# Splitting the second-half query projection 288/224 instead of 256/256, with a new written order

## The chip, the cores and the metric

The kernel runs on one core of one Trainium2 chip. The metric is device time in microseconds; lower is better. The core has five engines that run side by side and wait for each other by semaphores: TensorE (PE, with PEld for its weight loads), VectorE (DVE), ScalarE (ACT), GpSimd (POOL) and SyncE (SP), which here only starts DMAs.

## What is computed

Two attention layers share one input and their outputs are mixed by a gate. Layer A is recurrent: the 2048 rows are cut into 64 segments of 32, each is joined with 8 memory rows, and the first 8 rows of its output are the memory of the next segment.

```python
for s in range(64):                       # A: S=2048, Dm=512, H=32, Dh=128, M=8
    h = concat([mem, x[:, 32*s:32*s+32]])         # 40 rows
    q, k, v = h @ Wq, h @ Wk, h @ Wv              # 32 heads of 128
    p = softmax(where(mask, q @ k.T * Dh**-0.5, -1e9))
    o = (p @ v) @ Wo
    mem = o[:, :8]; outs.append(o[:, 8:])
# B: 4 blocks of 512 rows, 32 heads of 16: causal softmax attention in the block,
#    mixed with a linear-attention memory carried from block to block
g = sigmoid((x * gate_w).sum(-1))
return g * a + (1 - g) * b
```

The memory chains the 64 segments of A one behind the other. B does not wait for A, and fills gaps.

## The kernel before

**Work of a segment.** `p_seg(s)` records the operations of one segment. Heads come in two halves, r = 0 and r = 1, of 16 heads. `project(kind, r, ...)` records a projection through `wproj` (line L1391): for each of 4 chunks of the 512 input features it issues 4 matmuls, which work side by side on four 32-column strips of the array, with the same 32 rows of `h` (24 new rows and the 8 of the memory) as weights and up to 512 columns of the weight matrix streaming. The result, 128 partitions by up to 512 columns in one PSUM bank, is evicted to a buffer `st` in bf16 (`copy`, line L997, on ACT or DVE). For keys and queries `ktr` then turns 32x32 blocks on DVE (line L1447) into `KT` and `QT`. Values are evicted to `V_sb` alone.

The queries of half 1 are the one projection in two pieces: `two` gives the column ranges, and the names of the second piece's operations end in b: q1 and q1b on PE, their evictions, their transposes. Each piece has its own PSUM bank, eviction and transpose, and can be ordered apart from the other.

The rest of a segment, for each half r:

- H (a mask, 224 columns, line L1020) and S (scores, L1462 and L1466) into one bank; S_1 reads KT and both pieces of QT of half 1.
- exp on ACT (L1470), U (sums over keys, L1485), ln and rc on ACT (L1489, L1491: the reciprocal as exp of minus ln), then nrm on DVE (L1493) and nrr on DVE or POOL (L1496), which scale the probabilities.
- PV (L1527, L1532) and eviction of O into `OT_sb` (L997, `OTev`).
- wo, 8 steps of output projection (L1296), their eviction `par`, fold (a small matmul), and `hm` on DVE (L1319), which writes the memory rows of the next segment's `h`.

**Work beside it.** The other 8 rows of each segment, which depend on no memory, are projected for four segments at a time (rv, rk, rq of groups j, also L1391, with `xr` as weights). Each goes through one of three staging buffers `stg`; the values take a way through DRAM (rvst, L1363: `rest_v<-stg`). A projection's first matmul also waits until its staging buffer is free. Their output projection is wor (L1296, `OTr_sb`). Layer B has its own logits (bL, L1137), exponentials (bE, L1155), masks (bM, POOL), values (bPV, L1178) and tail (brow, `fin`, output DMAs). Pieces of its logits share four PSUM banks with the PV of half 1. `blast` is the last row block's B product.

**What sets the order.** Operations are recorded with their reads and writes and a set of candidate engines. The order of each engine's instructions is not found when the kernel is built: `ORDER`, a compressed string, lists for each of PE, ACT, DVE, POOL and SP which operation comes next, and `schedule()` follows it (`sequences()`, `given()`). An operation that may run on ACT or DVE (every `copy`), or on DVE or POOL (nrr), runs where the list has it. PSUM banks are handed out in the course of that. Each engine runs its list strictly in order; an instruction waits for the operations that it depends on, and with it all that stand behind it. PE runs either with four column strips, four row strips or the whole array, operation by operation.

Of the kernel before, what the change touches and what calls it, by code (L numbers as in the profile page):

```python
# [15 lines left out]
    "c-nPZ2S5|o8~<J|$z?$jP_ZJ40xsNWRkRLp)veS~_o{nUaqoenYNd|4t#uU_RdJ!<#syWXsEGa@sMV^7KuCb(-u>UZth->rgmCxno4@b(eedCLt<2<IfOKZvG@C-U41d%r"  # L16
    "mcsZ=<2SC%GMMGpZ@~!d(}c*RDMfo``kr{tbb{q(So3eSy%*XP-d(hC_4rlR>aRX6PQ5f|Y5x}1=y|j1-QE_G1(R#^sc~)pr}^lEsqzP-DaWU1g(4;+bjI8jvktY+4#+;$"
    "DZSpAq>;tHpKG_jf8vMzlVYYCURDBA(W!yYy&&$dt4SRIPD96z;S1&QJpq#7_G!**?ra&JyZlI6hsJ%Uri8az+$JpTW|ONeZUEGK^%0=rtB_)qH^7Zx-zwL8WEhzA`eopQ"
    "R%N-`@Ja_T89%|3uORR_Tm<<3!2E-)Ex>~CbrtGsO?RLNLX0-g`*x_;t?(RBSyZx=aJbRt!Z!~(zi}>wK0cdOzfI&69HRv}SWP}T0IKDC0I~xVfzKaV;7XKBZUS^UYaOMq"
    "BF5Xqf(1Y$&sE7D252>@<^788239kJD!rbt^b8brKLZe@uqv!<n-thQwh#=tDg@B*FLjOkS8mJ$rNe@W0KZIP;uWYEmCXZCK=He(j0Ij){U3xDUT^j6B|ux(;+x%$Hz^08"  # L20
    "BnImXbY{&z{_-5Je6?AZ9iYxU)VpdWc<XY_A7UrJ>VH|Muqe2^07VHA<l|$tf(bwuJG(FzqT{lcx}3WY5L)?UTaMA^A)OpP$E?XwLm}uu{j$P$<o=&7x#s~QlXj+ZtTq>U"
    "&z=W58^e53n}3Nh!Lr4Nccus;o7^NT|ArQM4R;O8<rucuOHq<9Cpr852gb&LQg(sd@BIA^P&thyA@7)><;*&U%ku~MvjB$qsD~-5h`9}4liSbYtixS#h#%g2>nMP8h~e~#"
    "9G%%aPt9hQeP8Ki8Qtmy_m56f#z69Imv4Om{s<0BL<o5m7)uZXxjs4il0sm>CujX!*5%pX6X3F`fx^O+Eza{T$*51^pefW9=rqf|8dP);V4O>2b_@TMN(2E2mHmLUN+>de"
    "+N?I~xy<@^p<H};3XJ##V46$xvHRWX90(m`2b$tD7(Wp}5;(xNNw(i7y2Q?3s^2~tG03X7s4Qw(fgyL@tQ7#u3P{dbm-k92Rua_;j`OjBoPfq)El|b6kD9`@Fw^bM&93ju"
    "9v{Ln#OrrKPoK8X6dLab7ivwft7%Q3OwaN8#-(=|tkS-zF!omkLI=haaNhE~zP|?Ls0pBDnLS^ape8&aX3Teqo<?3jbxE#b2LUm`E8noMmps2sYDu%HYwz3kuX^s1eVe?("
    "^m|8>@FOjliM6>b5Z5(@O1G^(<n^IjinoA2M)eG!92hJzu$gtx4DQ(CW3tGjs-UNI@!Wd7=N#i0hVv~38uxXJip=5P%_S0-EUgCck4yD#2x)fx@s&gxDm|FJV9ZLR#jI|3"
    "jKI1HTzxiZPjz>+_QCpI(Zh&Gd0fN)nL`1dvN@p6@il3+1DBKm<*RF>GD6KTa<3Cpr$3)An#8eIz2bwn8QSj(wdO;+%kT}P$<nIBBWP*1qdO@Q&L=~g3o-GjM-icqZL{oV"
    "gO*t`+bWOmKX=g*SnA5|7zIGA*RX>W1|+{`&=DADNztrYIC|r|ZSIBlKvwI4tqTc+u{h70)Bpf0mlerF$h{Z8z}Ow+=V+II^lD~xI5LPSX0@?{3o4?YdoB9KXT?;=(-cC&"
    "2m*=Y*>h;<md>N=4`npyzTk*OD4OH_X^I(J31Ni8!_*sL6rl^K?~<LC-7^J-Fq~CuHRdbp-vkAMIvI=&)RkdH)H|WRomOW71bh9}fm3+pGCG0=6`QMxUMT}m+v*UzD?fBn"
    "!uUUX{Q26y`!S7T#WcdAY!O@Zw*1?!k24_vkg|Bkh#eCP=dYYe>TRt{cna*=e&ozq0rNU}o@RY?&d%X#vz9=kHe|XhC;;H)>Cx6=Qjb)yyZ~6%Y8y#-qThB9!SW_FF*V>="  # L30
    "nTnv??3Mqtku_fhW?gQDLghO+G1Ub$WAwWBWeKm+`ZgBBi{Q^bIg}6HLfz(P*`g=o(#=k{Na?IT@YgAl-O5i`+D5csW%osy&kc<6>%$f;FoL@`M1PDrvMcVaow;<#1okFE"
    "%hzq=nQzmf8zDmKUA|HN30MZK^3%O+?a9q#m#j*#zFQ?qSjabrl%eJsR44E@zpDzGzk`&g$%?M7wSN$N$0;Xj3yD}Susl`;7%b_kfb5WTwYeT>Z5EnEQU0sE1}I`bHbiC}"
    "N1LM}pZsf@&d3@hdp)fkNFtFQqCU{n6|O4)AG_-l`m)8unmif=)#k~hmu?)talG2LHV*DeiDBRw9Vr}ro<e2O+19~~qLmW}D?e&j_z3F6KZHeg!>6qQ_;F{SZ9haNopX^5"
    "=%4t@I0~=y&<yfxJ(rWyJ44H8fL*jCy}<nSEfU;D_v+k3p%<aD?G;h%7x=soYCg9&r~&(4&xjgqCvXA<vRG?{li!nAlmlmSg8-fczhOy5GAw*nl6J=u-71+0{7B`fg*Bw{"
    "wLZ5$nM?+)&y_7Ebw7_FkMKLRN(*~fs60LgUb^Bmfb_T)UZ?sBcs7=p2?em92q#1E6Lp1`D=8Ja0u>Ck<AVVl%|o6q(5z5a2M4))-ZNOgcO;=K>aak>GVW;zXlzB90L@)$"
    "d)|aMJ#KwKLiQac$~C;JHL*pOuipvImia(Y50GPO-kE$l;S9HmEitL~z+mmB!E905{poI30QM%tohP2qg&H~zX@s=cs*-N%^1^Fe%Wr2wqR7N%>GjfxAFQnKz+{&+JwUEJ"
    "emGh;-KvMrzIon+Yl`V)<0rSMoU)LqvYiObUQfzV-X}aj^pWzgf6;ZmK;~5PRW^gVRMYQYq@ZP_AlZcyxYp`Yr&Ddu`?f4m*dIwIFL~t`kFWt30MiB|19Uh$V-ZF%`@>s6"
    "Rp5re077?~El?Tn?F<RyFbe+`R%5i_S}H~@pjKK~7Fbo-ALmv!X`6op-*jl8y9#ZK*i_scZ1})}Y#{ahcQ1wRb9wkg=3g5%Q`^V)x54oQd<HdGmcw$e7LgFZMI|0ivZPZN"
    "u}ZL63<&Fv!*DWl8aDq37H^`7G!JM*M$3*jiuH66eGX{~s?iD3kY5fgW<M|~pT22d_C1WnM=DbdMeHX(u&$m*7iPDm8Ploh!a|Mpb&w3}29<wvi#5DA%)#rZNE1764QLG5"
    "mqFe{;wP0{O^hZib!6A2N?c$;{^t;|l@L7@pAqiT7@<tW1)}<&uLRwM0+FUpN>xO)2$~npr4(0#jA6)I!Pt!{(#tdj&FLDMSx*SN+5;8wby*Osqy?!{keSlrP^+205o>9~"  # L40
    "r=jvD3J6*?Y8@#HgAk^rvsk1ncyRPMr*Qa1#Utv$sCb0DyPdN?Mm?DE2%d2Y?@tx%nW&oy2ya?R#3Or5NQ4Cx4TSq#Tz`h9jL5SwaxW8Z)-9fK`9w8nO*0alb`hmEmW1*<"
    "c;HAXH3KZfj*)|56vq<jRHcbr&>qLLQTO9?5pmJFbUA4BgvSMk?3dIeQFZ7%<W02MNEkM%#{#tBX8cUoteBNqiR!al?uM{-+nf3jO(EmRsG7v_7{1<n2xnz=G9@SrH8vVC"
    "11`%YcD7^0+r|inlrN}AXiG<tM9P4~Xx7iGr)y0$?1`r?RDDb{kcbCyEXUd7ZBmkS&g(arV+{82&|r8KES*=6aaci2dlE*($3Yrti&Y@Y;J`D{dHVUI^EB8qf3ZVN4cap>"
    "79na^>?rEIio&$1Gb48Ksf|H%93~(i0gqYc7D6CD)~HMvjiFxBl!Rm>2r3qm=}n$ow}1u`*KUQc+b<ANf7K;0)Bd;%_d6#_Ia#HhMcM`lcdmg3hg!N~SwRgly}IL7<%Oo&"
    "hZj{1jxweO+`=Oi)((k=um=ve8)XqdRm5I@^mfOB!XgSkQkdlix4J!(v68h40i>cDW)(nLMDs1IpzziDR@xtTLL7zNlSnE~<Kc|Ua9USh2Vu5I5?R7xBU%Sj44?Bu>~NyX"
    "$}nz8gb>x?@5?cEFc=8YYVbl-zI|=kt){nXKT*B&tCh^Qkk{T4^QrSGZDG2l$yTU$C{R9fI}|_fpPKpVmn|{tC$1-T;yv*0j5X61g7!|zi*Ap5XN7JZzSB0v6gNC4;zHYm"
    "le-o*g_dJ>-mCy`89xqc{Hy=0&+va8<eS^<dR-L(HfZvE@ITkThe{{RnOgsjUioEIQ0&El0bgvcl&6zH`@?k1npyPg4@Ol9<6oE@2|ixiMuQR~n^7hQnc-j`omEFDgxfjP"
    "Xl3O%?fV1Y{{ayYXf%^mtz%m<a-8f7t)aXZW-)qE2d+j~<+AxLqK-zvm58b=M@pWHo(8M8WBUA=yQ}vN*td04XH1&x!gW*D#=eYY_z9bDbV!N}VX>+}4V;lJQCx@wZ)ljy"
    "V&$9|@Xj;H<wIfE!7^*q=AQjxa0w#bz1^^W;vfB@S~D#cK!?OGCwsvWh*sGc<?F9dSk~hj^2HGAqk8R6no-z82J(HaD!t0@omm~knw1c-sR_Q-@^Vuq-?%Ni&CM97r2+*#"
    "q`>UmS`V_j|CD(oe)y%Qdyh1kxtus=^TA<v<mX^@(%IzAa0p<=Pt#evdMft8i<XzD^pI6sts<%Cu+ge5QR|~u*Tp5Ifu=$mkTHoqO{(r^-t~h6sf}k6Jr*_oHzenEqZ0MP"  # L50
    "k7xgdL5HCRUb4)*Y#C>;D&_Zb$87GJ&^5J9{)s8;rmUL|K(t%6K4{RMo5S*SN`zlSEfP)UEOa^@oqZ5`kH1dCIoX)IW7z`c*whyz&wU!PBZQhW?aE^!u}PX928<iafePcA"
    "nkU1_XhV8)+oXU7cN#+9KHj5gL=j%Hrg0iD<G1J`ac3s1jOMf)$;QP<=4>Yj?y&_XS<cyAT(XGyVdtE;aQI&Pf2!fSj{xfa75*^ze{#lKTL|If*H79493j<xN&f#t$QLy0"
    "bb>*jf7tdz9AxZOJq@Bo`nndwbUV53n}}&^{+RDQZJDA-weD<!vD!B~<rgEfANSJk=~;^+%4VFnY2234L!0Z>-~HaivTSa#7X97x%BFGEf;w%*C6}PXl$}SSDiWaV9s*mY"
    "li*ixw|#yre0P(>#M`+`jDzE>s`=YYC?Z)^?%yC1g9p_i^Xr<wfp<;jTC3-Kx8=h0qpVd%l&x5i+E6B!!|lkBtZ1?sFwb92yuA%y%VAs1mb&OQ30*1(Fj+pGfK)YMgC5Gu"
    "bYRs80AZMmz%f0Jbw3vPd=Xt$u=-~>-I+Pr{Y3eQxV|A!Okt}p`!1s{mIIUXtTh6*`m-ve+8#E!)qqS|f!S%TF13dE(OR<KRgl<|B!g^p#aH`LKz5)CI5ozbXIXW)<X+>G"
    "fciq5-#b`9RlO=NlqXYO)n!6hazubo=Ub--LpE-j`c)y^8ij4tO5^nwjNJS1cSaUt7Gb>%82O}K=)&*64NVEZikhcl99y)Ulzxr3N288J%?^vkHj=Fvuek(9i<c~Zt2OO2"
    "ej0F#)|miymbub8rdjudE`FqXDO_$Q!~k=r@$JZAyA&i=2y-+ta=nl2ec7tdMkf+uH_ir`9Lvx50`d?6uFW_-hGpcTh8DT|K^x)_L`=KV<^t*{hZF5WfZH^UgLl<n-sG>W"
    "bJyq@n{TckefAYV4eQgo_gc%%pebMRPJ{Hu)J-T+DX{fy*OV65BGH8~|306=XfxSbC8}-o$P{2~mmWWMEjrSF$DYM4C(Z-yt*<XBj{FLZKfLnQ<_2P5Y&GlMk-x%8ZT&16"
    "HPMi#tgnXAYM@rn-G{<ckFGMluL#Y5%v43MjBFHEHa6(@CDr>XN*Yahdm$n`{QK4yZytL;4X=%w!?g<v7&h-X$Tv>7HE3Ggg-ust^|eOU*fj28%GI`m8%!A1^0Eo9o*OZH"
    "=30nM+K}2jX3?(sul^aTM0MVQeD>|6SN-I}THi?cwx8~N=iqMb(9lCio+w*i?C^E9$AhMFKG3n@{gY_q>ka2vWusuU|H;zOC+BbMwuIGhbtQw_t+<xgC?#=G+L~IshBqDm"  # L60
    "+s~Pu+N2y#+S%vOz}o9O;A%k;IA#2{<j67B&+M{&KX(oKxoi6>Z|Y{^p(FlIeRp_3<TY+6`)d`&^m}L8Co&sYB|0~CP)c~3GO>MyFjh6V-tKy^qhSzSg^5psgV>-|(WmNO"
    "-Dy$zU%JrI|EqMgW>q+Q1x0Mw9J<js1cil0?M)q%)sdZY>EW2_nf<~;8+2?x_EP(>pITk&8NW+eedM&H9S!fS!W)`wnA@>=#t7JQAmD(tDqOqVbzV5ZP2CsgBbHrgQ{i}@"
    "L-XN(7dw2@<ZjCj3u``_)bH&jMxA!^uMMHCXLeJLX?5B3dlXw8?|_Km+uO2!gY=6hLF$!--_Ax=$HMbSR@Dqoxm-Ljd<+Dq*L!p|q20H*%k=KY1EvJLGC-Y&_0yx1>#vf@"
    "WNU?ej2T=zF7h>)zHNLvd)J^bTXw_1lC-tsn;+;lWPe}T!KfZb51)%jHgCb1*`52q9BqF4t%0yL!L)&`{BS{J+eO>o7r)pV*r|X2h;qu}7l}u!ZHaBSs$z8TrO(|WtNh?y"
# [517 lines left out]
class Kernel:  # L582
# [821 lines left out]
    def p_seg(self, s):  # L1404
# [97 lines left out]
        k0 = project("k", 0, pK)  # L1502
        q0 = project("q", 0, pK)
        k1 = project("k", 1, pQ)
        two = ((0, 256), (256, 512))
        q1 = project("q", 1, pQ, two)
        ktr("k", 0, k0, pK)
        ktr("q", 0, q0, pK)
# [84 lines left out]
```

## Time and profile before

| | |
|---|---|
| median of 3 runs | 833.93 us (832.82 to 835.31) |
| profiled execution, its own time | 833.41 us |
| its span, first to last instruction | 831.7 us |
| PE busy | 806.6 us, 97% |
| DVE busy | 616.6 us, 74% |
| ACT busy | 567.1 us, 68% |
| POOL busy | 252.8 us, 30% |
| granted TensorE clock | 1.00 |
| DMA moved | 45.62 MB |

The profile is of one execution. Busy time counts the union of an engine's instructions; matmuls are pipelined, and four that run side by side overlap, so the mean time of one matmul is not what it adds. The chain that ended last is followed back from the last instruction to what released it each time. A group line gives engine, operation, tiles and shape, the count, busy time and mean of one, and after the second bar the engine's idle time just before, with what ended it.

### The profile page before, as it was taken

The page shows a single profiled execution, that of the slowest core. Times are in us where ns is not written, and L with a number is a line of the kernel's source. Part 1 is how long each engine was busy: PE and PEld are TensorE (multiplying, and loading weights), DVE is VectorE, ACT ScalarE, POOL GpSimd, SP SyncE. Part 2 cuts the span into 40 slices and gives each one's busy share as a digit, 9 for nine tenths or more (in the row PEclk, how much of TensorE's full clock was granted, in tenths as well). Part 3 has the DMA queues.
Part 4 walks back from the last instruction along what each step waited for, and adds up shares of the span by engine and source line. Part 5 has one row for each costly group of instructions (what it writes and reads, how often), then busy time and mean ns, then how long its engine had stood idle before and what let it go on. Part 6 is the DMA issues. An engine that isn't in the chain of part 4 may idle for free.

```text
span 831.7 us, 53258 instructions
## 1 busy us (share of the span) xinstructions
PE 806.6 (97%) x24457; PEld 525.3 (63%) x24474; DVE 616.6 (74%) x1407; ACT 567.1 (68%) x1279; POOL 252.8 (30%) x567
## 2 busy tenths in 40 slices
PE   9989999999999999999999999999999999999987
PEld 4445666666666566666667666666756665766654
DVE  4768677778778767678787777877768777875776
ACT  3666766787667767767667677677656767767663
POOL 3443231234322233222332333423312313332440
PEclk9999999999999999999999999999999999999999
DMA  9983101211111210211022101100211110000001
GB/s 340 415 244 66 38 24 40 41 44 24 45 32 25 39 28 17 50 34 44 25 40 45 37 24 34 38 22 11 51 34 33 32 33 10 14 26 21 21 18 36
DMA packets 71700, 45.62 MB, mean 55 GB/s; under 512 B 50046, under 2 KB 69942, under 8 KB 69942
## 3 DMA queue, kind: packets, MB, share of 16 engines
q1 hardware_dynamic: 70422, 41.18, 17.6%
q8 instruction: 192, 3.15, 1.6%
q10 hardware_dynamic: 1056, 1.05, 0.4%
q14 instruction: 30, 0.25, 0.1%
HBM read 30.72 MB, written 8.87 MB: 48 GB/s over the span
## 4 chain that ended last, share of the span: by engine, by line
PE 85%; DMA 5%; ACT 3%; DVE 2%; SPq 2%; issue 1%; POOL 1%; DVEq 0%; POOLq 0%; ACTq 0%
PE pb L1391 47%; PE pb L1296 16%; PE pb L1020 7%; PE pb L1137 3%; DMA Wq_sb<-in_A_Wq_dram 3%; PE pb L1527 3%; PE pb L1178 2%; PE pb L1022 2%; PE pb L1485 2%; PE pb L1462 2%; DMA rest_v<-stg 1%; SPq L893 1%; PE pb L1226 1%; ACT rc_sb L1489 1%; PE pb L1466 1%
## 5 line engine op out<-in xcount | busy, mean ns | idle before, releaser
L997 ACT ACTIVATE st<-pb 128x512 bf16<-128x512 f32 (+2 forms) x309 | 148.8, 496 | 105.4 <-PE pb L1391 87.1
L1155 ACT ACTIVATE PTB<-pb 128x640 bf16<-128x640 f32 x240 | 158.2, 705 | 36.9 <-PE pb L1137 33.2
L1391 PE MATMUL pb<-Wv_sb,hT 128*32 128x512 bf16 x2048 | 161.5, 379 | 0.3 <-issue 0.3
L1391 PE MATMUL pb<-Wq_sb,hT 128*32 128x256 bf16 (+1 forms) x3072 | 141.1, 308 | 0.0
L1391 PE MATMUL pb<-Wk_sb,hT 128*32 128x512 bf16 x2048 | 134.1, 379 | 1.3 <-DVE ao L1326 0.7
L1296 PE MATMUL pb<-Wo_sb,OT_sb 128*32 128x256 bf16 x4096 | 132.2, 273 | 1.8 <-issue 1.4
L1161 POOL TENSOR_SCALAR_AFFINE_SELECT PTB<-PTB 128x512 bf16<-128x512 bf16 x120 | 78.1, 650 | 117.5 <-ACT PTB L1155 111.4
L1391 PEld LDWEIGHTS pb<-Wq_sb,hT 128*32 128x32 bf16 x3072 | 86.0, 97 | 39.8 <-issue 1.9
L1296 PEld LDWEIGHTS pb<-Wo_sb,OT_sb 128*32 128x32 bf16 x4096 | 100.5, 96 | 16.7 <-ACT OT_sb L997 3.2
L1447 DVE STREAM_TRANSPOSE QT_sb<-st 128x256 bf16<-128x256 bf16 (+1 forms) x192 | 94.5, 511 | 14.4 <-ACT st L997 12.3
L1447 DVE STREAM_TRANSPOSE KT_sb<-st 128x512 bf16<-128x512 bf16 x128 | 89.7, 701 | 12.3 <-ACT st L997 10.5
L1496 POOL TENSOR_TENSOR PT_sb<-PT_sb,rc_sb 128x64 bf16<-128x64 bf16 x87 | 31.9, 367 | 195.5 <-ACT rc_sb L1491 190.8
L1391 PEld LDWEIGHTS pb<-Wk_sb,hT 128*32 128x32 bf16 x2048 | 59.4, 97 | 42.4 <-DVE hT L1319 1.5
L997 ACT ACTIVATE OT_sb<-pb 128x320 bf16<-128x320 f32 (+1 forms) x140 | 58.5, 430 | 40.3 <-PE pb L1532 39.2
L997 DVE CAST OT_sb<-pb 128x320 bf16<-128x320 f32 (+1 forms) x120 | 56.8, 478 | 27.8 <-PE pb L1532 26.6
L1319 DVE CAST hT<-pb 128x32 bf16<-128x32 f32 x63 | 12.1, 192 | 70.7 <-PE pb L1020 70.4
L1391 PEld LDWEIGHTS pb<-Wv_sb,hT 128*32 128x32 bf16 x2048 | 51.8, 96 | 16.5 <-issue 0.2
L1489 ACT ACTIVATE rc_sb<-pb 128x160 f32<-128x160 f32 x128 | 39.1, 306 | 32.9 <-PE pb L1485 31.6
L1470 ACT ACTIVATE PT_sb<-pb 128x224 bf16<-128x224 f32 x128 | 45.5, 356 | 15.7 <-PE pb L1466 11.7
L1493 DVE TENSOR_TENSOR PT_sb<-PT_sb,rc_sb 128x160 bf16<-128x160 bf16 x128 | 42.2, 330 | 7.5 <-ACT rc_sb L1491 5.9
L1391 PE MATMUL pb<-Wk_sb,xr 128*32 128x512 bf16 x512 | 44.4, 380 | 1.8 <-DMA rest_v<-stg 1.8
L997 ACT ACTIVATE V_sb<-pb 128x512 bf16<-128x512 f32 x76 | 45.0, 592 | 1.7 <-PE pb L1391 1.2
(202 smaller groups left out, 1464.3 us busy)
## 6 DMA issues: line engine op xcount, KB each, us to landing
Wv_sb<-in_A_Wv_dram SPq DMA_DIRECT2D x4, 1024.0 KB, 11.1
Wk_sb<-in_A_Wk_dram SPq DMA_DIRECT2D x4, 1024.0 KB, 21.4
Wq_sb<-in_A_Wq_dram SPq DMA_DIRECT2D x4, 1024.0 KB, 27.0
Wo_sb<-in_A_Wo_dram SPq DMA_DIRECT2D x4, 1024.0 KB, 21.4
rem_v<-rest_v SPq DMA_DIRECT2D x63, 64.0 KB, 3.1
rest_v<-stg SPq DMA_DIRECT2D x28, 128.0 KB
a_rows<-ao SPq DMA_DIRECT2D x63, 32.0 KB
stg<-a_rows SPq DMA_DIRECT2D x15, 128.0 KB
```

What stands on the lines that cost most here:

```text
L997: self.P.op(("act", "dve"), (lambda a: a.activation(dst, src(), ACT.Copy), lambda d: d.tensor_copy(dst, src())), reads=reads, writes=write ...
L1020: ins = pe.matmul(out[32 * c:32 * c + 32], lhsT[:, 32 * c:32 * c + 32], rhs, start=start, stop=stop, tile_position=(0, 32 * c), **kw)
L1137: ins = pe.matmul(pb[slot.banks[i]][:, base + a - lo:base + b - lo], KT[r0:r1, 128 * kc:128 * kc + 128], Q[r0:r1, t0 + a:t0 + b], start=Tr ...
L1155: P.op("act", (lambda dst=dst, src=src: lambda a: a.activation(dst, src(), ACT.Exp, scale=0.25))(), reads=[pair], writes=["%s%d_%d" % (nam ...
L1161: P.op("gp", (lambda pt=pt, ii=ii: (lambda g: g.affine_select(pt, pt, ([[0, len(ii)]] if len(ii) > 1 else []) + [[1, 128]], ALU.is_ge, 0.0 ...
L1296: ins = pe.matmul(pb[so.b][p0:p0 + 32, 0:256], tok(r, g, l), self.Wo[:, h, 256 * d:256 * d + 256], start=(r == 0 and g == 0 and l < 2), st ...
L1391: ins = pe.matmul(self.pb[sl.b][32 * g:32 * g + 32, 0:hi - lo], x[:, c, 0:32], cols, start=(c == 0), stop=(c == C - 1), tile_position=(0, ...
L1447: op("dve", (lambda dst=dst, src=src: lambda d: d.transpose(dst, src))(), reads=["st%d%s" % (i, tag)], writes=["%sT%d%s" % (kind, r, tag)] ...
L1470: op("act", lambda a: a.activation(PT[:, r, :], pb[rb.b][:, 0:224], ACT.Exp, scale=SCALE), reads=[rb], writes=["PT%d" % r, "PT%dr" % r], n ...
L1489: op("act", lambda a: a.activation(rc[:, r, :], pb[rb.b][:, 0:160], ACT.Ln), reads=[rb], writes=[rr], name="ln%d_%d" % (s, r), cost=t_act( ...
L1493: op("dve", lambda d: d.tensor_tensor(PT[:, r, 0:160], PT[:, r, 0:160], rc[:, r, :], ALU.mult), reads=[rp, rr], writes=[rp], name="nrm%d_% ...
L1496: op(("dve", "gp"), tuple((lambda e: e.tensor_tensor(rest, rest, late(rc[:, r, :]), ALU.mult)) for _ in range(2)), reads=[rp + "r", rr], w ...
```

## The change

The second half's queries are cut at column 288 instead of 256, so that the first piece has 9 blocks of 32 columns and the second 7. Number of matmuls, evictions and transposes are the same. All else in the code is the same but `ORDER`, which is a new string: it orders the same 6472 operations anew on PE, ACT, DVE and POOL, and puts some that have a choice of engine on the other one. SP's order is the same.

```diff
 ORDER = (
-    "c-nPZ2S5|o8~<J|$z?$jP_ZJ40xsNWRkRLp)veS~_o{nUaqoenYNd|4t#uU_RdJ!<#syWXsEGa@sMV^7KuCb(-u>UZth->rgmCxno4@b(eedCLt<2<IfOKZvG@C-U41d%r"
...
+    "c-nnh2V7Iv_dho;$;%`RaVsb|QGV8~s09&i-BpXNqmI^HwOXxOMXe%g)uL9dtByK~v)0LUAcz|WP8=0lH=+^}Nb>Ic-}jQd+!y@(<0tFoymQa^p6@yL;z$jH)o)b>#divY"
...
 )
...
         k1 = project("k", 1, pQ)
-        two = ((0, 256), (256, 512))
+        two = ((0, 288), (288, 512))
         q1 = project("q", 1, pQ, two)
```

Operations by engine, where the list moves some: ACT 1284 to 1269, DVE 1407 to 1410, POOL 563 to 575. By kind, on DVE before and after: value evictions 52 and 61, query evictions 40 and 44, key evictions 21 and 19, evictions of O 120 and 125, nrr 41 and 35 (the rest of nrr, 87 and 93, on POOL).

## The prediction

> **What bounds the kernel now.** I read the page first: its busy shares, the chain that ended last, and the groups by shape.
>
> ```profile
> span 831.7 us, 53258 instructions
> PE 806.6 (97%) x24457; PEld 525.3 (63%) x24474; DVE 616.6 (74%) x1407; ACT 567.1 (68%) x1279; POOL 252.8 (30%) x567
> PE 85%; DMA 5%; ACT 3%; DVE 2%; SPq 2%; issue 1%; POOL 1%; DVEq 0%; POOLq 0%; ACTq 0%
> ```
>
> TensorE (PE) is busy for 806.6 of 831.7 us and carries 85% of the chain. No other engine is near its limit, so the end moves only with PE's own work or with the 25.1 us in which PE waits. The windows say where those lie:
>
> ```profile
> 0.00:60.00 60.00, 54.04 (x974) 27.28 (x980) 39.91 (x104) 33.06 (x65) 27.40 (x75) 1.00 0.94 343
> 60.00:800.00 740.00, 726.92 (x22714) 482.41 (x22727) 556.15 (x1257) 521.46 (x1181) 219.38 (x480) 1.00 0.14 32
> 800.00:831.70 31.70, 25.60 (x780) 15.64 (x769) 20.58 (x47) 12.61 (x35) 6.04 (x13) 1.00 0.11 32
> ```
>
> The columns are length, then PE, PEld, DVE, ACT, POOL busy, the clock, the DMA share. PE idles 6.0 us while weights arrive (DMA share 0.94), 13.1 us in the 740 us of segments, 6.1 us in the tail. The clock is full throughout. Next, what the edited steps cost, by shape, and who waits for the scores that use them (line L1462):
>
> ```profile
> L1391 PE MATMUL pb<-Wq_sb,hT 128*32 128x256 bf16 x2048 | 77.2, 273 | 0.0
> L1447 DVE STREAM_TRANSPOSE QT_sb<-st 128x256 bf16<-128x256 bf16 x128 | 50.5, 415 | 3.5 <-ACT st L997 2.7
> L1447 DVE STREAM_TRANSPOSE QT_sb<-st 128x512 bf16<-128x512 bf16 x64 | 45.0, 703 | 11.0 <-ACT st L997 9.6
> L997 ACT ACTIVATE st<-pb 128x256 bf16<-128x256 f32 x99 | 37.5, 384 | 12.4 <-PE pb L1391 10.3 <-PE pb L1020 0.8 <-DVE KT_sb L1447 0.3
> L997 DVE CAST st<-pb 128x256 bf16<-128x256 f32 x29 | 11.5, 401 | 1.4 <-PE pb L1391 1.2
> ...
>   DVE QT_sb L1447: 4.9, 20
> ```
>
> The last line is from the scores' own view: weight loads for scores waited 20 times, 4.9 us in all, for a transpose of queries. Matmuls in flight cover those waits: the same view puts PE's own idle time before the scores at 0.3 us, once. Last, the chain around a stall of the common kind (start, length, what):
>
> ```profile
> 511.62 0.10 PE pb L1466 x4
> ...
> 511.74 0.36 ACT PT_sb L1470
> 512.10 0.49 ACT V_sb L997
> ...
> 512.60 0.31 ACT rc_sb L1489
> ...
> 512.93 0.34 ACT rc_sb L1491
> 513.27 0.56 ACT stg L997
> ```
>
> After the scores of half 1, ACT does the exponential, a V eviction, logarithm, reciprocal and another eviction in a row, and PE's next logits wait for the last. PE's waits are ends of such queues on ACT and DVE, not the query halves.
>
> **The 288/224 pieces.** PE: in segment 30 the first matmuls of the two halves start at 420.628 and 421.064 us, 0.436 for sixteen, so 0.109 for four of 256 columns; four of 512 take 0.216. Between these, 0.418 ns a column gives 0.122 for 288; four 224-column matmuls of H start 0.096 before S. A pair is 0.218 either way: nothing, times 4 contraction steps and 64 segments. Evictions: ACT 384 ns at 256 and 599 at 512 (its 128x512 row) is 0.84 ns a column, so 411 and 357; DVE 401 and 682 gives 436 and 366. Transposes: 415 and 703 give 451 and 379. Each pair sums to what it did, the counts are equal. Only latency moves: the 288 piece reaches QT_sb 32 x (0.84 + 1.125) = 63 ns later after its matmuls, the 224 piece 63 ns sooner.
>
> It counts only where the piece is last before S_1. By the written order the last of k1, q1 and q1b on PE is q1b in 29 segments before and 30 after, q1 in 21 and 16, k1 in 14 and 18. If each paid or gained in full: (16 - 30) x 0.063 = -0.9 us. Starts of S beyond their usual step sum to only 1.2 us in the trace (over 0.1 us each, 5 cases), so the bounds are -0.9 and +1.0 (sixteen late pieces, none gaining). I take -0.2, nearest to that 0.3 us of idle.
>
> **The new order.** All engines but SP are reordered. Of PE's 2914 steps 1578 keep their predecessor and 1661 their very place; most of the rest move by one to four places. So I counted what stands between.
> - Changes of PE's tile mode from column to row groups: 166 before, 164 after. In the trace the step ahead of each exceeds its usual length by 21.9/166 = 0.13 us: -0.3.
> - PE work between the last of k1, q1, q1b and S_1: under 1.45 us in 13 segments before, 7 after. ACT instructions between exp and ln of half 0: 39 before, 26 after (query evictions 17 and 8); nrr ahead of nrm on DVE in half 0: 14 and 6. These shorten the chain from S_0 to PV_0, which V matmuls mostly cover. Thirteen evictions of 0.38 fewer, all on the path, would be -4.9; all covered, 0; a loss is the slower rival's. I take -0.8, near the covered end, since S and U together wait 2.1 us beyond their usual steps.
> - The largest single wait past the start:
>
> ```profile
> 607.51 5.39 DMA rest_v<-stg
> 612.90 0.04 issue
> 612.94 0.83 PE pb L1391 x12
> ```
>
> rk12_0 waits for the staging store of rv12_0; PE idles 1.64 us. After, rvev12_0 is behind ln45_1 (0.31), and rq12_0 (four steps, 0.86) no longer has its first step ahead of rk12_0 (0.22): +0.5. Bounds: hidden, -1.6; the store a further eviction (0.60) late, +1.1.
> - Tail: `blast` moves from ahead of wo63_0, where 0.25 us of issue precede it, into the softmax of segment 63, and q63_1 runs ahead of the wait that ended at 818.72 after the output store: -0.2 and -0.3, bounds 0 and -1.0.
> - Untouched: bL6_6, bL7_7, bL10_6, bL11_7 and PV61 have almost the same queues in front of them, the row at 511.62 included; I leave those stalls. In the first 60 us SP's order is the same and DMA sets the pace: 0.
>
> Sum: 0 - 0.2 - 0.3 - 0.8 + 0.5 - 0.5 = -1.3 on the profiled execution's 833.4 us (span 831.7): 832.1. That execution lies 0.5 below the median of 833.9; taken between, I say 832.4. A measurement tells 0.3% (2.5 us) from no change, so this counts as none.
>
> **Rivals.** Slower: DVE becomes the late one. V evictions on DVE go from 52 to 61 (684 ns), of O from 120 to 125 (485), second-half queries' and others' shift too, about +7 us net. In half 1, 11 segments have under 1.2 us of PE work between U_1 and PV_1, where ln 0.31, rc 0.34 and nrm 0.33 already need 0.97. A V eviction in front of nrm costs PE some 0.35, half of itself. From 10 such places it passes 2.5 us; at 14, +4.9: 837.3. For it: half of PE's steps have new neighbours. Against: a V eviction directly ahead of nrm in half 1 goes only from 4 to 5. Chance 0.27.
>
> Faster: the shorter queues on ACT in half 0 work through. If a third of the 13.1 us of mid-kernel idle goes, -4.4: 829.0; at half, 827. For it: 39 to 26, 13 to 7. Against: the large waits are of half 1 and stay. Chance 0.27.
>
> That the uneven split does nothing at all is inside the forecast: without it, 832.6.
>
> A smaller one: POOL and DVE hold each other up. POOL gets 12 more operations (nrr 87 to 93, others +6). nrm on DVE (line L1493) ran 284 to 471 ns, 325 median beside a POOL operation, 319 otherwise; nrr on POOL took 305 to 592, 375 beside a two-input DVE operation, 307 otherwise. Twelve at +0.2 is 2.4, and 3.5 with the sum's gains lost: 835 to 837, chance 0.02. The Trainium skill ("SBUF — State Buffer", Who interferes with whom) has the rule: a DVE instruction with two SBUF inputs contends with a GpSimd one that reads SBUF, and the later one blocks for the other's whole length; the spread agrees in direction, the medians show far less than a full block.
>
> **How the numbers follow.** Forecast 0.44, own range 830 to 835.5: 0.12 of it under 831.4 (faster by over 0.3% of 833.9), 0.31 inside, 0.01 above 836.4. With the faster rival faster is 0.39; same 0.31; slower 0.27 + 0.02 + 0.01 = 0.30. Both signs hold much, so the range runs from half the idle gone (827.5) to the slower rival with 17 places (838.5).
>
> **What would show it.** PE busy within 2 us of 806.6; 128x288 rows near 411 and 451 ns, 128x224 near 357 and 379; the query entry under the scores' waits at or below 4.9 us; a wait of 1.5 to 2.5 us before rk12_0; PE idle between 60 and 800 near 12. Wrong if PE idle there rises past 16 with DVE `V_sb` or `PT_sb` ahead of PV, or falls under 9, or if a 288 piece costs PE a step longer than 0.125.

## The result and the profile after

The change made the kernel slower: a median of 836.99 us (834.46 to 844.48, 20 runs) against 833.3 us (829.55 to 837.6, 20 runs) on the same chip, a ratio of 1.0056 (1.0039 to 1.0072). The forecast was 832.4. The profiled execution took 836.28 us, 2.9 more than that of before.

The first lines of the page and the share of the chain:

```profile
span 834.5 us, 53238 instructions
...
PE 807.4 (97%) x24441; PEld 521.2 (62%) x24459; DVE 622.6 (75%) x1410; ACT 559.5 (67%) x1264; POOL 257.8 (31%) x579
...
PE 87%; DMA 4%; DVE 3%; ACT 3%; issue 2%; SPq 1%; POOL 0%; DVEq 0%; POOLq 0%
```

PE's work is what it was (807.4 against 806.6). One share of the chain has grown that the prediction had passed over: "issue" (1% before, 2% after), time in which PE waits for nothing that the profile shows. The same three windows as before:

```profile
0.00:60.00 60.00, 54.39 (x973) 27.69 (x980) 39.96 (x103) 32.94 (x65) 28.38 (x77) 1.00 0.97 345
60.00:800.00 740.00, 724.77 (x22577) 475.40 (x22591) 558.34 (x1254) 511.18 (x1157) 221.68 (x486) 1.00 0.14 32
800.00:834.50 34.50, 28.25 (x895) 18.12 (x888) 24.34 (x54) 15.36 (x43) 7.73 (x17) 1.00 0.11 31
```

PE idles 15.2 us in the middle stretch (before 13.1), 6.2 in the tail (6.1). Busy time alone misleads here, though: a matmul at half clock is busy twice as long. The window of the segments' start shows that (before, the clock was 1.00 throughout):

```profile
58.00:60.00 2.00, 1.26 (x49) 0.96 (x47) 1.53 (x3) 1.30 (x2) 0.70 (x2) 1.00 0.55 99
60.00:62.00 2.00, 0.52 (x7) 0.34 (x9) 0.09 (x1) 0.00 (x0) 0.14 (x1) 0.81 0.32 70
62.00:64.00 2.00, 1.67 (x19) 0.54 (x13) 0.80 (x3) 0.84 (x2) 0.00 (x0) 0.50 0.03 8
64.00:66.00 2.00, 2.00 (x57) 1.62 (x59) 0.56 (x2) 0.46 (x1) 0.64 (x1) 0.84 0.00 0
```

From 61.24 us on, for 3.41 us, the granted clock is 0.50. What comes before it is on the chain. Before, around the last output step of segment 0 (wo0_7, line L1296):

```profile
58.61 0.11 PE pb L1296 x4
58.72 1.45 issue
60.16 0.29 PE pb L1296 x4
...
61.31 1.05 PE pb L1022 x13
```

and after:

```profile
58.83 0.43 PE pb L1296 x14
59.26 2.22 issue
61.48 0.40 PE pb L1296 x2
...
63.45 1.64 PE pb L1022 x13
```

PE stops in the middle of wo0_7, for no semaphore, 0.8 us longer than before, and the thirteen matmuls of L1022 then take 1.64 us instead of 1.05. From the start of wo0_7 to the start of the same step of segment 1 the changed kernel loses 2.0 us.

**What "issue" is.** The page counts packets of instructions that were fetched. Queue 8 has the same line in both kernels:

```profile
q8 instruction: 192, 3.15, 1.6%
```

192 packets and 3.15 MB are 16 KB each, and PE's 24457 matmuls and 24474 weight loads are 255 to a packet. PE's stops of this kind recur at instructions that are a multiple of 256 apart, and six of them stand at the same instruction number in both kernels. I read a packet as one block of 256 PE instructions, and call it a crossing when PE starts the first instruction of a block. After a crossing, the packet of the next block starts 0.92 us later (median after 62 us in nine traces; over 1.83 in one case of twenty) and takes 1.05 us, and where PE had to wait, it goes on some 1.4 us after the packet has landed: 3.4 us in all, 4.2 in one of twenty. PE needs a median of 4.05 us for a block in before and 4.10 in after, so the next is mostly there in time, but a block that PE runs through quickly, or a packet that starts late, makes PE stop. Late packets are the commoner: of the 117 stops after 62 us in these traces 60% have a packet that started over 1.5 us after the crossing, as 11% of all blocks do. In the two traces here, up to 56 us, beside the weights' transfers (DMA share 0.94 and 0.97 over the first 60 us), the packet starts 2.0 to 5.3 us after the crossing. The packet for which wo0_7 stopped started at 56.7 us before and at 58.9 us after, 2.0 and 3.6 us after its crossing.

I call a stop a gap of over 0.3 us at such a boundary, at an instruction that waits for no semaphore, and count it in sums less the usual 0.11 us; a single stop is given as the whole gap from start to start (2.49 us for wo0_7 after, where the chain shows 2.22). Before has 8, 5.25 us in all; after has 14, 8.85 us. That is 3.6 us for a span that is 2.9 longer. One that both have, in an output projection of the other rows (wor) behind that of segment 43, before and after:

```profile
587.11 0.21 PE pb L1296 x5
587.32 0.25 issue
587.56 0.51 PE pb L1296 x11
```

```profile
591.84 0.11 PE pb L1296 x2
591.95 0.96 issue
592.90 0.61 PE pb L1296 x14
```

From its first to its last instruction the block took 3.05 us before and 3.12 after; the packet started 1.25 us after the crossing before, 2.05 after. Here the packet differed, and hardly the block.

### The profile page after: what moved, and what is told of

It reads as the page before. It is cut to its first block, busy times and chain, and to the rows that moved or that the text cites. A ratio compares the mean times of both kernels' runs of the same rounds, so it can differ in the third digit from the quotient of the medians.

```text
span 834.5 us, 53238 instructions
## 1 busy us (share of the span) xinstructions
PE 807.4 (97%) x24441; PEld 521.2 (62%) x24459; DVE 622.6 (75%) x1410; ACT 559.5 (67%) x1264; POOL 257.8 (31%) x579
## 3 DMA queue, kind: packets, MB, share of 16 engines
q8 instruction: 192, 3.15, 1.6%
q10 hardware_dynamic: 1056, 1.05, 0.4%
## 4 chain that ended last, share of the span: by engine, by line
PE 87%; DMA 4%; DVE 3%; ACT 3%; issue 2%; SPq 1%; POOL 0%; DVEq 0%; POOLq 0%
PE pb L1391 48%; PE pb L1296 16%; PE pb L1020 7%; PE pb L1137 4%; PE pb L1527 2%; PE pb L1022 2%; PE pb L1178 2%; PE pb L1485 2%; DMA st<-in_A_mem_dram 2%; DMA rest_v<-stg 2%; PE pb L1462 1%; PE pb L1226 1%; ACT rc_sb L1489 1%; PE pb L1466 1%; ACT rc_sb L1491 1%
## 5 line engine op out<-in xcount | busy, mean ns | idle before, releaser
L997 ACT ACTIVATE st<-pb 128x512 bf16<-128x512 f32 (+3 forms) x306 | 145.7, 494 | 113.6 <-PE pb L1391 97.3
L1391 PE MATMUL pb<-Wq_sb,hT 128*32 128x512 bf16 (+2 forms) x3072 | 140.5, 308 | 0.2
L1296 PE MATMUL pb<-Wo_sb,OT_sb 128*32 128x256 bf16 x4096 | 131.2, 273 | 2.6 <-issue 2.2
L1296 PEld LDWEIGHTS pb<-Wo_sb,OT_sb 128*32 128x32 bf16 x4096 | 101.2, 96 | 16.3 <-ACT OT_sb L997 3.7
L1391 PEld LDWEIGHTS pb<-Wq_sb,hT 128*32 128x32 bf16 x3072 | 84.3, 97 | 41.9 <-issue 2.5
L1496 POOL TENSOR_TENSOR PT_sb<-PT_sb,rc_sb 128x64 bf16<-128x64 bf16 x93 | 34.3, 369 | 245.3 <-ACT rc_sb L1491 241.9
L1447 DVE STREAM_TRANSPOSE QT_sb<-st 128x288 bf16<-128x288 bf16 (+2 forms) x192 | 94.3, 508 | 5.6 <-ACT st L997 3.5
L997 DVE CAST OT_sb<-pb 128x320 bf16<-128x320 f32 (+1 forms) x125 | 59.4, 482 | 30.7 <-PE pb L1532 29.2
L997 ACT ACTIVATE OT_sb<-pb 128x320 bf16<-128x320 f32 (+1 forms) x135 | 55.8, 427 | 39.1 <-PE pb L1532 37.8
L1493 DVE TENSOR_TENSOR PT_sb<-PT_sb,rc_sb 128x160 bf16<-128x160 bf16 x128 | 44.8, 350 | 14.2 <-ACT rc_sb L1491 13.0
L997 DVE CAST V_sb<-pb 128x512 bf16<-128x512 f32 x61 | 41.6, 683 | 8.1 <-PE pb L1391 6.9
```

What stands on the lines that cost most here:

```text
L997: self.P.op(("act", "dve"), (lambda a: a.activation(dst, src(), ACT.Copy), lambda d: d.tensor_copy(dst, src())), reads=reads, writes=write ...
L1296: ins = pe.matmul(pb[so.b][p0:p0 + 32, 0:256], tok(r, g, l), self.Wo[:, h, 256 * d:256 * d + 256], start=(r == 0 and g == 0 and l < 2), st ...
L1391: ins = pe.matmul(self.pb[sl.b][32 * g:32 * g + 32, 0:hi - lo], x[:, c, 0:32], cols, start=(c == 0), stop=(c == C - 1), tile_position=(0, ...
L1447: op("dve", (lambda dst=dst, src=src: lambda d: d.transpose(dst, src))(), reads=["st%d%s" % (i, tag)], writes=["%sT%d%s" % (kind, r, tag)] ...
L1493: op("dve", lambda d: d.tensor_tensor(PT[:, r, 0:160], PT[:, r, 0:160], rc[:, r, :], ALU.mult), reads=[rp, rr], writes=[rp], name="nrm%d_% ...
L1496: op(("dve", "gp"), tuple((lambda e: e.tensor_tensor(rest, rest, late(rc[:, r, :]), ALU.mult)) for _ in range(2)), reads=[rp + "r", rr], w ...
```

## The experiments

The theory that came out of the two traces: the widths cost nothing; the new order costs time through what lies between two block boundaries, at wo0_7 (with the half clock) and in the segments. Rivals: the 288-wide piece; the order's waits for ACT and DVE, wherever the blocks lie. Each time below stands against the kernel before, measured beside it on the same chip.

**The parts of the change.** Only the widths, in the old order:

```diff
-        two = ((0, 256), (256, 512))
+        two = ((0, 288), (288, 512))
```

> The old order with the pieces 288 and 224; engines, PSUM banks and order are those of the kernel before. If the uneven pieces cost the time (a 288-column step dearer than it looks, or a later transpose): +2 to +4 us on the kernel before. If the order does: within 0.7 us of the kernel before.

Measured 834.23 us (12 runs) against 834.35, ratio 1.0000 (0.9990 to 1.0011). The widths cost and bring nothing. One thing that the expectation states was not so: 191 operations got another PSUM bank, since banks are handed out by planned times (`cost` in the code) and these follow the widths; order and engines were those of before.

Only the order. These two lines alone gave no program to time; with a few more edits, not shown, the planner's costs stay those of 288 and 224 columns, so that the banks too are those of the changed kernel:

```diff
-        two = ((0, 288), (288, 512))
+        two = ((0, 256), (256, 512))
```

> The new order with the second-half queries still in two pieces of 256; every instruction stands where the changed kernel has it, only the widths of the two pieces differ. Theory (the order alone costs the time, the widths nothing): 836 to 838 us, 3 to 4 us over the kernel before, with the stop of over 2 us at the last piece of segment 0's output projection (wo0_7, near 59 us). Rival (the 288-wide piece costs time only together with the new order): 833.5 to 835 us.

Measured 839.19 us (6 runs) against 834.89, ratio 1.006 (1.0039 to 1.0082). 18 stops, 11.1 us in all, the longest of 2.97 in wo0_7, and the half clock after it. The order alone loses the time.

**Where in the order.** `ORDER` spliced of both lists, 288/224 in both kernels: up to the end of segment 1 (74 us in the planner's time, the "head") from one list, the rest from the other. The diff is in words:

```diff
-ORDER = (all of the new list)
+ORDER = (old list up to 74 us, new list from there)     # oldhead
+ORDER = (new list up to 74 us, old list from there)     # newhead
```

> The changed kernel with the old order up to the output projection of segment 1 (about the first 77 us), the new one from there on, pieces 288 and 224. If the loss sits at the start (PE's 2.2 us without instructions at 59 us and the half clock for 3.4 us behind it): +0 to +1.5 us on the kernel before. If it is spread over the segments: +2.5 to +4.

Measured 838.45 us (6 runs), ratio 1.0061 (1.0039 to 1.0082). The longest stop of the head was 0.69 us and the clock 1.00 or 0.999 in all runs, so the head was mended; the segments lost it again, with 14 stops of 8.6 us after 62 us (after: 9, 4.65).

> The reverse: the new order up to the output projection of segment 1, the old one from there on, pieces 288 and 224. If the loss sits at the start: +2 to +4 us on the kernel before, with the half clock in the profile of about every second run. If it is spread over the segments: within 1 us of the kernel before.

Measured 838.38 us (8 runs), ratio 1.0045 (1.0029 to 1.0061). The stop in wo0_7 is 2.87 us, followed by 6.83 us at half clock, and the old order behind it now stops 14 times for 6.4 us instead of 6 times for 3.3. Splicing was no clean cut: 395 operations (old head, against after) and 707 (new head, against before) got another PSUM bank, and what lay between two boundaries changed too. Each hybrid loses about what the whole new order does: by what was expected, the first says that the loss is spread and the second that it sits at the start. So this pair does not tell where it sits.

**Moving the boundaries, not the order.** The kernel waits for its first data in the first microseconds and keeps PE running with 24 warm-up matmuls of 512 columns. Cut in four, they have the same columns, but each adds six instructions (three weight loads and three matmuls), and every later block begins that much earlier in the work. Nothing else moves: order, engines, banks and waits stay.

```diff
-                return pe.matmul(pb[sw.b][:, 0:512], self.phiK[:, 0, :], self.phiQ, start=True, stop=True)
+                w = 128 if i < 12 else 512
+                for j in range(0, 512, 512 if isinstance(pe, Count) else w):
+                    ins = pe.matmul(pb[sw.b][:, j:j + w], self.phiK[:, 0, :], self.phiQ[:, j:j + w], start=True, stop=True)
+                return ins
```

> The kernel before, its order and all its work as they were, but 12 of the 24 warm-up matmuls of the first 16 us are cut into four of 128 columns: 72 more TensorE instructions ahead of everything else, no more columns. So every later block of 256 instructions begins 72 instructions earlier in the work. Theory (TensorE stops where a block of 256 instructions is run through faster than the next is fetched, and what an order costs is which instructions come to lie in one block): from the starts of the instructions in the trace of before, with the stops taken out, the sum over blocks of what each is shorter than 3.45 us (5.2 us before 62 us) is 2.5 us as it stands and 8.5 us with the boundaries 72 earlier; measured stops of 5.3 us should rise to 10 to 13 us and the time by 4 to 8 us, to 838 to 842 us. Rival (the stops come from the order's waits or its transfers, not from where the blocks lie): within 1 us of the kernel before, 833.5 to 835.5 us.

Measured 850.2 us (845.59 to 851.45, 5 runs) against 834.89, ratio 1.0172 (1.0148 to 1.0196). Twelve matmuls cut in four cost 15 us, about twice what I had expected. In the trace there are 28 stops, 16.4 us, all after 62 us and most of them a multiple of 768 instructions apart, about a segment's number: what falls badly in one segment does so in the next.

> The changed kernel with 12 warm-up matmuls cut into four: 72 more TensorE instructions in the first 16 us, order and columns as they were. Theory (what the order costs is decided by where the blocks of 256 instructions lie in it, for either order): the kernel before lost 15 us at this shift, so the changed one should lose about as much, with 20 to 30 stops at block boundaries that sum to 14 to 20 us: 845 to 852 us. No boundary in wo0_7, so no stop over 2 us near 59 us and no half clock. Rival (the new order is worse by itself and the shift hits the old order by chance): 835 to 839 us.

Measured 859.19 us (855.03 to 860.37, 5 runs), ratio 1.0277 (1.0255 to 1.0299), more than expected again: 47 stops, 30.4 us, the longest before 62 us of 1.34. There was no half clock behind wo0_7, but one from 25.3 to 28.7 us, which the expectation had not foreseen. In the page and the waits of PE the loss stands plainly:

```profile
span 857.5 us, 53309 instructions
...
PE 87%; issue 4%; DVE 3%; ACT 3%; DMA 3%; SPq 1%; POOL 0%; DVEq 0%; POOLq 0%
```

```profile
PE pb L1023 <- issue: 8.3, 14, 1.0
PE pb L1299 <- issue: 7.8, 15, 1.5
PE pb L1394 <- issue: 4.3, 8, 1.2
PE pb L1530 <- POOL PT_sb L1499: 1.5, 3, 1.0
PE pb L1140 <- ACT V_sb L1000: 1.5, 3, 0.5
```

(columns: engine and line, what it waited for, us in all, times, longest; lines are three further down than in the changed kernel). These waits for POOL and ACT are the changed kernel's own to a tenth; what has grown much is "issue". So the boundaries matter for either order, and much more than the whole change.

All 24 cut in four, and eight filler matmuls (which keep PE running while weights arrive) in two, is 208 instructions. Which eight of the 24 fillers V0 and V2 differs between the two kernels:

```diff
+                w = 128
...
+                def f_fill(pe, m, sw=sw, part=part, w=256 if (k, c, i) in (...) else 512):
```

> The kernel before with all 24 warm-up matmuls cut into four and eight filler matmuls of the first 26 us cut into two: 208 more TensorE instructions, no more columns, the order as it was. Theory of the blocks: the same sum is 2.0 us instead of 2.5 us, so 833 to 835 us, no change that can be told or up to 1 us less. Rival (more instructions in the first 26 us cost time of themselves): 1 to 4 us more. This is the control for the next kernel and for the 72.

Measured 832.56 us (828.68 to 834.56, 12 runs), ratio 0.9966 (0.9950 to 0.9983): faster than the kernel before and than the 833 to 835 expected. The profiled run, 834.34, is among its longest; it has 13 stops, 9.1 us, which my sum (2.0) had not foreseen.

> The changed kernel with the same 208 more TensorE instructions in the first 27 us, its order as it was. Theory of the blocks: the sum over blocks is 1.2 us instead of 2.8 us, no block boundary lies in wo0_7, so the stop of 2.5 us there and the half clock after it go; 833 to 835 us, 2 to 4 us less than the changed kernel and level with the kernel before. Rival (the new order's waits for other engines cost the time, wherever the blocks lie): 836 to 838 us, as the changed kernel.

Measured 839.78 us (834.87 to 843.69, 12 runs), ratio 1.0054 (1.0033 to 1.0076). A miss: the clock was 1.00 or 0.999 in every run, so the half clock did go, but PE still stopped for 1.98 us at the boundary behind wo0_7 and for 7.35 in the segments. Of those 14 blocks 13 were not short (3.6 to 4.2 us, one 3.2); their packets started 1.2 to 2.4 us after the crossing, and the one for the first stop took 3.3 us. A sum over short blocks with one fixed time for the fetch does not foretell such stops.

**The first 60 us alone.** With 72 instructions in front, and 184 more in the value projections of segments 1 to 4, the boundaries lie from about 115 us on one whole block further, that is where they lay (`CUT` names the projections):

```diff
...
+                        step = 256 if 0 < c < self.CUT.get(name, 0) and not isinstance(pe, Count) else hi - lo
+                        for j in range(0, hi - lo, step):
+                            ins = pe.matmul(self.pb[sl.b][32 * g:32 * g + 32, j:j + step], x[:, c, 0:32], cols[:, j:j + step] ...
...
```

> The changed kernel with the 72 more instructions in the first 16 us, and 184 more in the value projections of segments 1 to 4 (second to fourth chunk in two matmuls of 256 columns instead of one of 512), so that from about 115 us on the blocks lie where the changed kernel has them (256 later, one whole block). It tells the share of the first 60 us apart. Theory (half of the loss is the late block in wo0_7 and the half clock behind it): stops before 62 us fall from 4.2 us to under 1.5 us, no half clock, and the time to 833 to 835 us. Rival (the loss is all in the steady segments): 836 to 837.5 us.

Measured 836.62 us (833.47 to 840.39, 12 runs) against 835.39, ratio 1.0023 (1.0008 to 1.0038): between the two expectations. The clock was 0.997 or 0.998 in 3 of 12 runs, the profiled one among them, so the head was mended in most runs and not in all; after 62 us the trace has 8.3 us of stops, where after has 4.65.

> The kernel before with the same two edits, so that only its first 115 us have other block boundaries. Stops before 62 us should go from 1.95 us to about 0 (as they did with the 72 alone): 831 to 834 us. Rival (the 184 more instructions in the value projections cost of themselves): 835 us or more; this is the control for the kernel above.

Measured 834.51 us (12 runs), ratio 0.9994 (0.9983 to 1.0004). No stop before 62 us, as expected, but 7.1 us of them later, where before has 3.3, and no gain; the edit by itself costs nothing.

> The kernel before with the 72 in the first 16 us and 136 more in the value projections of segments 1 to 4: the first 60 us as in the run with 72, which had no stop there, and from about 115 us on the boundaries of the run with 208. If both shares add up, 830 to 832.5 us, the fastest of all; if the place of the boundaries is chance from run to run, 832 to 835 us.

Measured 829.72 us (828.03 to 833.29, 6 runs) against 835.39, ratio 0.9943 (0.9925 to 0.9962): the fastest of all, beating both kernels, with the order of before and 256-wide pieces. Its trace has 5 stops, 2.55 us, none before 62 us. The page's span and chain, and PE's waits:

```profile
span 827.5 us, 53465 instructions
...
PE 86%; DMA 4%; ACT 4%; DVE 3%; issue 1%; POOL 1%; SPq 1%; DVEq 0%; ACTq 0%; POOLq 0%
```

```profile
PE pb L1398 <- DMA rest_v<-stg: 2.0, 2, 1.7
PE pb L1534 <- POOL PT_sb L1503: 1.9, 4, 0.9
...
PE pb L1025 <- issue: 1.0, 6, 0.2
```

Lines are up to seven further down than in the kernel before. Its waits for other engines are much those of before (two of 1.2 and 0.9 us, for DVE, are new); "issue" is no longer among the first.

> The changed kernel with the 72 more instructions in the first 16 us and 160 more in the value projections of segments 1 to 4, so that from about 115 us on the boundaries lie 232 instructions earlier. From the starts in three traces of the new order and the times of block fetches in nine traces (median 3.4 us from a crossing to the next block's readiness, 4.2 us in one of twenty), the stops after 62 us should come to 6.7 to 8.3 us at this place against 8.6 to 10.4 us where the changed kernel has them. Theory (the new order's loss is where the blocks lie, and there is a place for them at which it is level with the kernel before or better): 831 to 835 us. Rival (the new order has more fast stretches wherever the boundaries are): 836 to 840 us.

Measured 836.37 us (12 runs) against 833.24, ratio 1.0041 (1.0022 to 1.0060). The rival's number: the head was mended in this trace (one stop of 0.34 us before 62 us; the clock was 0.998 in 3 of 12 runs), but 12 stops of 8.7 us came after it.

**All together.** Each kernel's span in its profiled run, the stops in it, and the difference:

| kernel | span | stops, us | span less stops |
|---|---|---|---|
| before | 831.7 | 5.25 | 826.4 |
| after | 834.5 | 8.85 | 825.7 |
| widths only | 831.2 | 6.40 | 824.8 |
| order only | 837.2 | 11.13 | 826.1 |
| old head, new rest | 835.4 | 9.52 | 825.9 |
| new head, old rest | 838.6 | 9.81 | 828.8 |
| before, 72 / 208 | 843.8 / 832.6 | 16.41 / 9.10 | 827.4 / 823.5 |
| after, 72 / 208 | 857.5 / 833.9 | 30.41 / 9.22 | 827.0 / 824.7 |
| before, head / head and 208 | 832.7 / 827.5 | 7.06 / 2.55 | 825.7 / 825.0 |
| after, head / head and 232 | 838.2 / 834.8 | 10.12 / 8.91 | 828.1 / 825.9 |

Stops differ by 28 us, what is left by 5. Five of these runs have the half clock inside: 6.83 us of it in the new head, 3.41 us in after, order only, after with 72 and after with the head moved. With half of that taken off too, the six runs of the old order leave 823.5 to 827.4 us, 825.5 in the mean, and the six of the new one 824.0 to 826.4, 825.1. Without stops and half clock the new order is level with the old one.

What stays open: why the new order stopped longer than the old one in the pairs at 0 and 72 and with the head mended. At 0, with two traces each at the same boundaries, the old order has 5.25 and 6.40 us, the new one 8.85 and 11.13. After 62 us it has 15 blocks under 3.45 us against 11, too few to say it by that, and packets start late in both. At 208 the two profiled runs have the same stops, but one is among the longest of its kernel's runs and the other among the shortest. Nor does the place of a boundary settle whether PE stops there. Three pairs of kernels have the same order and the same boundaries from about 115 us on; from 118 us on their traces have 5 stops of 3.0 us and 13 of 6.5 (before, and with its head moved), 8 of 3.9 and 10 of 8.0 (the same of after), and 8 of 6.3 and 4 of 2.3 (before with 208, and with head and 208), with one stop in common in the last pair. That other transfers hold up the packets is suggested by the contrast of the first 56 us with the rest, and not without exception: in the old order with the 72 in front, a packet at 53 us started 0.5 us after the crossing beside fully busy DMA engines. Later the start follows the DMA's load weakly (median 1.23 us where over 12 of the 16 engines were busy in the half microsecond before the usual start, 0.86 where none was). So the loss is shown to be stops at block boundaries, with the half clock, and these are shown to depend on where the boundaries lie, though not on that alone; no place was found at which the new order beats the old one, nor is it shown that there is none.

## Why the prediction was wrong

**The pieces: right.** By shape, in the profile after:

```profile
L1391 PE MATMUL pb<-Wq_sb,hT 128*32 128x288 bf16 x1024 | 44.3, 286 | 0.0
...
L1391 PE MATMUL pb<-Wq_sb,hT 128*32 128x224 bf16 x1024 | 37.7, 259 | 0.0
...
L1447 DVE STREAM_TRANSPOSE QT_sb<-st 128x288 bf16<-128x288 bf16 x64 | 28.5, 445 | 0.3
...
L1447 DVE STREAM_TRANSPOSE QT_sb<-st 128x224 bf16<-128x224 bf16 x64 | 24.2, 379 | 0.2
...
L997 ACT ACTIVATE st<-pb 128x288 bf16<-128x288 f32 x50 | 20.5, 410 | 4.0 <-PE pb L1391 3.4 <-DVE KT_sb L1447 0.2
...
L997 ACT ACTIVATE st<-pb 128x224 bf16<-128x224 f32 x49 | 17.4, 356 | 6.0 <-PE pb L1391 5.0 <-DVE KT_sb L1447 0.8
```

445 and 379 ns of transpose (451 and 379 foretold), 410 and 356 of eviction (411 and 357). The scores' view has the query wait at 3.1 us, 13 times, where at most 4.9 was foretold:

```profile
  DVE QT_sb L1447: 3.1, 13
```

**"In the first 60 us SP's order is the same and DMA sets the pace: 0": this step failed.** SP's order is the same, but PE was not paced by its weights alone. PE's reordered work crossed into the block ahead of the stop 0.6 us later than before, the packet behind it started 2.2 us later, and PE stopped 0.8 us longer and then ran 3.41 us at half clock, which is 1.7 us of work: 2.0 us lost by segment 1. Why the packet started so much later is not shown. The Trainium skill ("TensorE: Matmul & The Clock Gate", What's actually happening) has the rule that an idle window of about 3.4 us halves the clock. The trace agrees in length (3.41 us at half clock), but PE was not idle in front of it: it was busy for 1.43 of the 3.41 us before. In the 20 runs of after, the 9 with a granted clock of 1.000 over the run average 835.8 us, the 9 at 0.997 or 0.998 838.0, and the 2 at 0.996 842.7. So the half clock goes with about 2 us in half of the runs, and 2.5 us are lost without it.

**A term that was missing.** The sum forecast -1.3 us and had no term for "issue" beyond 0.25 us in the tail. It read PE's waits as ends of queues on ACT and DVE, though the waits of PE in the profile before name "issue" among the first:

```profile
PE pb L1391 <- DMA rest_v<-stg: 1.8, 2, 1.6
PE pb L1296 <- issue: 1.7, 2, 1.4
```

and after, at their head:

```profile
PE pb L1296 <- issue: 3.2, 2, 2.2
```

The code names it as well: the planner has BLOCK = 256 and FETCH = 3.6 (lines 183 and 185) and counts such stops. The term was worth +3.6 us in the two profiled runs. Its size could hardly have been foretold, though: the sum over short blocks that the later expectations use gives 2.5 us for the old order and 2.8 for the new one, 0.3 apart. The Trainium skill ("Runtime: NRT & Kernel Launch", Instruction fetch mechanics) says that PE's instructions come in blocks of 256 and that crossing into the next is mostly hidden. The traces agree on the blocks; "mostly hidden" holds for most of the 192 of them and still leaves 2.6 to 30 us, since PE needs 4.05 us for a block here and the fetch 3.4 to 4.2.

**The other terms of the order.** The -0.3 for mode switches did not come: steps ahead of one exceed their usual length by 23.6 us in 164 places, against 21.9 in 166. The -0.8 for shorter chains of half 0 did not come in the places named: all excess of U over its usual step sums to 3.1 us instead of 2.3, that of S to 1.90 instead of 1.84. rk12_0's wait was to grow by 0.5 and fell, from 1.64 (the longest of the rest_v row shown above) to 0.98:

```profile
PE pb L1391 <- DMA rest_v<-stg: 1.2, 2, 1.0
...
PE pb L1527 <- DVE PT_sb L1496: 0.7, 2, 0.4
PE pb L1137 <- ACT OT_sb L997: 0.6, 1, 0.6
```

The tail's idle time was to fall by 0.5 and stayed (6.2 and 6.1), though from segment 58 to 63 the distance to before fell by 1.3 us. Taken together, span less stops and less the 1.7 us of half clock went from 826.4 to 824.0, the way of the forecast sum; but runs of the old order alone spread from 823.5 to 827.4 by this measure, so the -1.3 is neither shown nor refuted for the work it looked at.

**The rivals.** "Slower: DVE becomes the late one" had the sign and not the mechanism: 0.7 us in two waits of PV for nrr on DVE and 0.5 in two for nrm are all that PV lost to DVE's scaling of the probabilities. That its 837.3 us lies beside the measured 837.0 is luck. The faster rival did not occur: PE's idle time in the middle rose. POOL against DVE did not show: PV waits for POOL 1.5 us, 1.9 before. The sign of being wrong, PE idle past 16 us with DVE `V_sb` or `PT_sb` ahead of PV, did not occur either, at 15.2; the prediction's list of signs had none for what happened.

## What to carry to other kernels

Where the bounding engine runs many small instructions, divide its instructions by 256 and compare the time of a block with the time of a fetch (here 4.05 against 3.4 to 4.2 us) before pricing a reordering: if they are close, any edit that adds, drops or moves instructions shifts stops by more than its own worth. Look for "issue" in the engine's waits, see whether the places are a multiple of 256 instructions apart, and before judging an order on such a kernel, run it at two or three positions of the boundaries (a few harmless instructions in front), several times each. The cheapest gain here was of that kind: 0.57% from splitting matmuls that compute the same.

## What was unexpected of the hardware

- Cutting twelve warm-up matmuls in four, with no more columns and the same order behind, made the old order 1.7% slower and the new one 2.2% (1.0277 over 1.0056); another number of instructions made the old one 0.34% faster, and 0.57% with the head's boundaries moved apart from the rest's.
- A block's packet starts soon after PE enters the block before it, 0.92 us after in the median, and 2.0 to 5.3 us after in the first 56 us of the two kernels, where the DMA share was near 1; there was no sign of more than one block in hand.
- After a stop of 2.2 us with few matmuls around it the clock was halved for 3.41 us; in the new head and old rest for 6.83 us, twice that. In after with 72 it was halved at 25.3 us, where PE had been busy for 2.35 of the 3.40 us before and no stop of that kind had come.
